# Who evicts the first scores, where expert 0's second weights load, and a new written order

## The chip, the cores and the metric

The kernel runs on one core of a Trainium2 chip. The core has a matmul engine (TensorE, PE in the profile; PEld are its weight loads), VectorE (DVE), ScalarE (ACT), GpSimd (POOL) and SyncE (SP), each with an instruction stream of its own, and 16 DMA engines. The metric is the device time of one execution in microseconds (us). A measurement is the median of several executions; the profile shows one execution by itself.

## The reference

Two blocks follow each other. The first is DeltaNet attention: for 4 x 8 heads of width 48 a state is carried over 768 positions. The second is a mixture of experts over the 3072 rows of 384 that come out: each row goes to the one of 8 experts with the largest logit.

```python
for t in range(S):
    kt, vt, bt = (k_n[:, :, t], v[:, :, t], beta[:, :, t, None])
    y[:, :, t] = np.einsum('bhd,bhde->bhe', q[:, :, t], state)
    v_old = np.einsum('bhde,bhd->bhe', state, kt)
    state = state + bt[:, :, :, None] * np.einsum('bhd,bhe->bhde', kt, vt - v_old)
...
logits = x @ w_gate
expert_idx = np.argmax(logits, axis=1)
...
for e in range(E):
    ...
    h = np.maximum(x_sorted[lo:hi] @ w1[e], 0.0)
    y_sorted[lo:hi] = h @ w2[e]
return (gate_w[:, None] * y).astype(np.float32)
```

k_n is k divided by its norm, gate_w the softmax weight of the chosen expert. All is float32.

## The kernel before

**Attention.** The 768 positions are cut into 12 tiles of 64; the work on one tile is a turn, t = 0 to 11. Within a tile the recurrence is solved by the inverse of a triangular matrix. `scores` (L373) makes the products of keys with keys (into XY, a part of blkA) and with queries (into P, a part of pA), and ScalarE evicts them (L309). Tiles 0 and 1 are handled apart: their products of keys are evicted first into GD, four copies of 32 partitions for each tile, by ScalarE for tile 0 and by VectorE for tile 1 (L311). For the later tiles SP copies GD from XY by DMA. VectorE multiplies P by a mask (L412). `invert(n)` computes the inverses of tiles 2n and 2n+1, all on VectorE: it transposes GD (L437), takes the norms (L445 to L470), keeps their transposed form `nt` (L472), eliminates in steps (L486 to L509) and transposes the result into TT (L517).

A turn is a chain between TensorE and ScalarE. Before it ScalarE scales v by the norms (L530, 16 small instructions a tile, which need `nt`) and copies it to a bank ("pair<-v"). Then come the product of state and keys (L554 into the same bank), the copy to R, the inverse (L583), the copy to Z, the product across the halves (L593), R again, the inverse again (L583), Z again, the update of the state (L607) and its copies to S. Beside the chain stand the output of a tile (L554 with queries, and L639), its eviction to x, its write to HBM (xs), and the logits (L659 transposes, L669, L678, each with an eviction to xT, lgT, lg).

**Routing.** Tiles of 128 rows are routed in groups of 8, 8, 2, 4 and 2. VectorE finds the largest logit (L718 to L735), ScalarE the exponentials (`ex`, L722), TensorE the ranks (L743 and L747, into a bank from which VectorE reads `rk`, L752). `su` (L766) sums `ex`. `listed` turns ranks into the lists of rows of each expert (L796 to L821). With the lists of the first three groups the first 256 rows of expert 0 are gathered (`early_rows`, POOL) and computed early (`early`): transposes (L927), `hidden` (L945) and `second` (L977).

**Experts.** For each of 8 experts: gather, L927, eight blocks of `hidden` with the first weights w1, then `second` with the second weights w2, scaling and scatter. The weights lie in three buffers, taken from the memory of blkA and pA, and SP loads them in three DMAs for w1 and two for w2.

**What sets the order.** All instructions up to the end of the experts are given to a planner (`Plan`) with an engine, an estimated cost, a priority (lower goes first) and a latency. The planner plays the program through with these estimates and writes down the order in which each engine gets its instructions; every engine then works through its list in that order, and waits where an operand isn't there. The dependences that the planner is given only shape this order; the waits on the chip come from the tiles that an instruction reads and writes. The planner also puts in fillers (L1120), matmuls whose result nobody uses, where it expects TensorE to be idle. Constants on top of the file are its estimates and priorities: RUN is how far ahead of their turn the scores are, OUT and LOG how far behind it the output and the logits, MASK the priority of L412, L3 and L4 those of the last lists, APART the turn from which the logits use another bank, ENOUGH the amount of recent matmul work above which no filler is put in.

`cf` is one DMA with all constants, issued by ScalarE; `ents` is a small ScalarE copy of the row numbers out of it. Its latency is 2.5 in the planner.

Of the kernel before, what the change touches and what calls it, by code (L numbers as in the profile page):

```python
# [20 lines left out]
NT = S // C  # L21
# [7 lines left out]
NK = DM // 128  # L29
# [4 lines left out]
FAR = 1 << 20  # L34
RING = 6
AHEAD = 5
RUN = 4.75
PAGE, FILL, STALL = 125, 3.8, 0.8
OUT, LOG = 1.1, 0.2
LATER, OUTL = 8, 1.3  # L40
LISTS, L3, L4, TURN = 9.5, 20.2, 11.05, 11.0
APART = 5
VP, MASK = 0.5, 2.2
WINDOW, WAKE, STAY, PASS = 3.413, 1600, 1750, 8.5
FILLER, ENOUGH, FROM = 0.22, 2500, 36.0
SLACK = 2.0
URGENT = -70

# [170 lines left out]
def tile_kernel(ctx: ExitStack, tc: tile.TileContext, kq, ktok, vtok, betal, wgk, w1, w2, out):  # L219
    nc = tc.nc  # L220
    P = Plan()
# [8 lines left out]
    fc, where = _consts()  # L230
    cf = pool.tile([128, fc.shape[1]], FP32, name="cf")
# [30 lines left out]
    def kb(b):  # L262
        return [("bk", b), ("bk", b + 1)]
# [23 lines left out]
    GD = blk(8)  # L287
# [7 lines left out]
    def dma(eng, o, i):  # L295
        return lambda: eng.dma_start(out=o, in_=i)
# [10 lines left out]
    def copy(eng, o, i, scale=1.0):  # L307
        if eng == "ACT":
            return lambda: nc.scalar.activation(out=o, in_=i, func=AF.Copy, scale=scale)  # L309
        if scale == 1.0:  # L310
            return lambda: nc.vector.tensor_copy(out=o, in_=i)  # L311
        return lambda: nc.vector.tensor_scalar(out=o, in0=i, scalar1=scale, scalar2=None, op0=OP.mult)
# [3 lines left out]
    P.op("DVE", 0.1, lambda: nc.vector.memset(tiny[:], 0.0), w=["tiny"], prio=-99)  # L316
    P.op("ACT", 0.2, lambda: nc.scalar.activation(out=tiny[:], in_=tiny[:], func=AF.Copy), w=["tiny"], prio=-45)
    P.op("ACT", 0.5, dma(nc.scalar, bl[:], betal), w=["bl"], prio=-49, lat=2.5)
    P.op("ACT", 0.5, dma(nc.scalar, cf[:], nc.inline_tensor(fc, name="c_f32").ap()), w=["cf"], prio=-48, lat=2.5)
    P.op("DVE", 0.2, lambda: nc.vector.memset(wg[:], 0.0), w=["wg"], prio=-48)  # L320
    P.op("ACT", 0.5, dma(nc.scalar, wg[:, :, 0:E], wgk), w=["wg"], prio=-40, lat=2.5)
    P.op("DVE", 1.0, lambda: nc.vector.memset(pairs[0][:], 0.0), w=kb(BS), prio=-50)
# [8 lines left out]
    for i in (2, 3, 4, 5):  # L331
        P.op("POOL", 1.85, lambda i=i: nc.gpsimd.memset(kqA[:, 2048 * i : 2048 * i + 2048], 0.0),
             w=kKQ(i) + [("zero", i)], prio=-60)
    for e in range(2):
        r = slice(64 * e + D, 64 * e + 64)
        P.op("SP", 0.6, dma(nc.sync, kqA[r, 2048:4096], kqA[r, 10240:12288]), r=[("zero", 5)], w=[("zero", 1)],
             prio=-40, lat=2.5)
# [25 lines left out]
    def scores(t):  # L363
        v = KQ(t)
        n, u = divmod(t, 2)
        xy = XY[n % 3]

        def run(bank, ks, fs):
            w = C * len(ks)
            for i, f in enumerate(fs):  # L370
                for e in range(2):
                    for x in range(2):
                        nc.tensor.matmul(  # L373
                            bk[bank + e][half(x), i * w : i * w + w].rearrange("p (k c) -> p k c", c=C),
                            lhsT=v[feat(e), 0, x * FQ + f, :],
                            rhs=v[feat(e), ks[0] : ks[-1] + 1, x * FQ + f, :],
                            start=True, stop=True,
                        )

        if t < 2:  # L380
            b = (BY, BZ)[t]
            P.op("PE", 1.15, lambda: run(b, (0,), range(FQ)), r=kKQ(t, (0,)), w=kb(b), prio=t - 95, passes=64, use=770)

            for q in range(4):
                eng = ("ACT", "DVE")[u]
                o = GD[quad(q), :, 16 * u : 16 * u + 16].rearrange("p c (e f) -> p c e f", e=2)
                i = pairs[b // 2][quad(q)].rearrange("p e (f c) -> p c e f", c=C)[:, 32 * (q % 2) : 32 * (q % 2) + 32]
                P.op(eng, 0.5 if u == 0 else 0.6, copy(eng, o, i), r=kb(b), w=[("GD", q, u, e) for e in range(2)], prio=t - 94)
            P.op("ACT", 1.0, copy(
                "ACT",  # L390
                xy[:, :, 16 * u : 16 * u + 16].rearrange("p c (e f) -> p c e f", e=2),
                pairs[b // 2][:].rearrange("p e (f c) -> p c e f", c=C)),
                r=kb(b), w=[("XY", n % 3, u, g) for g in range(2)], prio=t - 60)
            if t == 1:
                P.op("ACT", 0.2, copy("ACT", cnt[:], const("first")), r=["cf"] + kXY(0), w=["cnt"], prio=-55)
            P.op("PE", 1.2, lambda: run(BY, (1,), range(FQ)), r=kKQ(t), w=kb(BY), prio=t - 50, passes=64, use=770)
            P.op("ACT", 1.0, copy("ACT", Pm(t).rearrange("p e f c -> p e (f c)"), pairs[3][:]),
                 r=kb(BY), w=[("P", t % RING)], prio=t - 50)
        else:
            for g in range(2):  # L400
                P.op("PE", 1.1, lambda g=g: run(BY, (0, 1), range(4 * g, 4 * g + 4)), r=kKQ(t), w=kb(BY),
                     prio=t - RUN + 0.01 * g, passes=32, use=770)
                src = pairs[3][:].rearrange("p e (f c) -> p e f c", f=4)
                P.op("ACT", 0.5, copy(
                    "ACT",
                    xy[:, :, 16 * u : 16 * u + 16].rearrange("p c (e f) -> p c e f", e=2)[:, :, :, 4 * g : 4 * g + 4],
                    src[:, :, :, 0:C].rearrange("p e f c -> p c e f")),
                    r=kb(BY), w=[("XY", n % 3, u, g)], prio=t - RUN)
                P.op("ACT", 0.5, copy("ACT", Pm(t)[:, :, 4 * g : 4 * g + 4, :], src[:, :, :, C:]),
                     r=kb(BY), w=[("P", t % RING)], prio=t - RUN)  # L410
        later = const("later").rearrange("p (e c) -> p e c", e=2).unsqueeze(2).to_broadcast([128, 2, FQ, C])
        dve(1024, lambda: nc.vector.tensor_tensor(out=Pm(t), in0=Pm(t), in1=later, op=OP.mult),  # L412
            ["cf"], [("P", t % RING)], t - MASK)
# [235 lines left out]
    def spare(t):  # L649

        return BZ if t < APART or t == NT - 3 else BY if t < NT - 2 else BS if t < NT - 1 else BZ

# [171 lines left out]
    def numbered(o, of, k, r, pr):  # L824

        n = of.shape[1]
        far = fars[:, 0:n]
        dve(n, lambda: nc.vector.tensor_scalar(
            out=far, in0=of, scalar1=0.0, scalar2=float(FAR), op0=OP.is_equal, op1=OP.mult), r, ["fars"], pr)
        dve(n, lambda: nc.vector.scalar_tensor_tensor(  # L830
            out=o, in0=of, scalar=-1.0, in1=far, op0=OP.add, op1=OP.add), r + ["fars"], [k], pr)
# [6 lines left out]
            a[:, NK * F :].rearrange("p (c d) -> p c d", c=NF),  # L838
        )

    def weights(e, pr, behind=()):
        i = e % 3
        a1, a2 = wview(i)
        extra = []
        if e == 0:
            extra = kXY(0) + kXY(1) + [("GL", k) for k in range(2)]
        if e == 1:
            extra = [("P", k) for k in range(RING)]
        if e == 2:
            extra = [k for i in range(2) for k in (("U", i), ("U", i, 21))] + [("GD", q, u, e) for q in range(4) for u in range(2) for e in range(2)] + kXY(2)  # L850
            extra += [("TT", k, h) for k in range(2) for h in range(2)]
        for s in range(NK):
            P.op("SP", SP(524288),
                 dma(nc.sync, a1[:, s, :], w1[e].rearrange("(s p) f -> p s f", p=128)[:, s, :]),
                 r=behind, w=[("w", i, s)] + extra, prio=pr + s)
        for h in range(2):
            P.op("SP", SP(786432),
                 dma(nc.sync, a2[:, 4 * h : 4 * h + 4, :],
                     w2[e].rearrange("(c p) d -> p c d", p=128)[:, 4 * h : 4 * h + 4, :]),
                 r=behind, w=[("w", i, 3 + h)] + extra, prio=pr + 3 + h)  # L860
# [128 lines left out]

    def early_rows():  # L990

        weights(0, 8)
        prepare(0)
        two_tiles = lst[:].rearrange("p (t e) o -> p t e o", e=E)[:, 0:2, 0, :]
        numbered(rows_ei[:], two_tiles[:, :, 0], "rows_ei", ["lst"], -74)
        dve(2, lambda: nc.vector.tensor_copy(out=rows_e[:], in_=two_tiles[:, :, 1]), ["lst"], ["rows_e"], -73)
        xv = XIN[0][0]
        for t in range(2):
            P.op("POOL", 1.0, lambda t=t: gather(xv[:, t * DM : t * DM + DM], rows_ei[:, t : t + 1]),
                 r=["rows_ei"] + [("xs", i) for i in range(18)], w=[("xin", 0, t)], prio=11, lat=2.5)  # L1000

    def early():
        xT, hT = parts(0, EARLY, 0)
        guard = [k for i in range(3) for k in kKQ(i)]
        turned_rows(0, (0, 1), xT, TURN, guard, (BR, BR + 1))
        hidden(0, xT, hT, 21, guard, (2, 0, 3, 1))
        for t in range(2):
            second(0, t, hT, 128 * t, (4, 6)[t], 21.2 + 0.01 * t)
            finish(t, (4, 6)[t], 128, rows_e[:, t : t + 1], rows_ei[:, t : t + 1], "rows_e", 21.2)
# [41 lines left out]
    for i in range(NT + AHEAD + 1):  # L1051
        t = i - AHEAD
# [26 lines left out]
        if i % 2 == 0 and 2 <= i <= NT:  # L1079
            invert(i // 2 - 1)  # L1080
            if i == 2:

                for j in range(2):
                    P.op("POOL", 1.4, lambda j=j: nc.gpsimd.memset(Sbs[j][:], 0.0), r=[("nt", 0)],
                         w=[("S", j, e) for e in range(2)], prio=-15)
                P.op("POOL", 1.85, lambda: nc.gpsimd.memset(kqA[:, 0:2048], 0.0), r=[("nt", 0)],
                     w=kKQ(0) + [("zero", 0)], prio=0)
                last_rows()
    prepare(1)
    numbered(rows_i[:], lst[:, :, 0], "rows_i", ["lst"], -74)  # L1090
    early()

    weights(1, 20, ["rows_i"])
# [125 lines left out]
```

## Time and profile before

| | |
|---|---|
| time, median of 3 runs | 532.78 us (531.04 to 533.56) |
| the profiled execution's own time | 526.99 us |
| its span, first to last instruction | 525.2 us |
| granted TensorE clock, mean | 0.952 |
| TensorE busy | 468.0 us (89%) |
| VectorE, ScalarE, GpSimd busy | 243.7, 191.0, 84.9 us |
| bytes moved by DMA | 63.84 MB |

The start of the first inverse (the first L583 of a turn) in the timeline, in us from the start of the span:

| turn | 0 | 1 | 2 | 3 | 4 | 5 |
|---|---|---|---|---|---|---|
| starts at | 42.52 | 58.09 | 77.27 | 90.50 | 107.29 | 123.42 |

| turn | 6 | 7 | 8 | 9 | 10 | 11 |
|---|---|---|---|---|---|---|
| starts at | 140.99 | 153.65 | 167.87 | 180.84 | 193.69 | 210.66 |

How to read it: busy times are those of one profiled execution, and so are all the times in the timeline. Matmuls overlap with the next one's weights, so a busy TensorE need not be at its peak. "Idle before" is the time in which an engine had nothing to do ahead of an instruction, with the one that released it; "issue" is time for which the profile shows no wait. A float32 matmul of the program appears as two rows in the trace, so counts in the timeline are twice those of the program.

### The profile page before, as it was taken

How to read it: one execution, taken by the hardware profiler on the slowest of the kernel's cores; microseconds unless marked ns; L12 is line 12 of the kernel's file. 1: busy time of each engine (PE TensorE's matmuls, PEld its weight loads, DVE VectorE, ACT ScalarE, POOL GpSimd, SP SyncE). 2: the span in 40 equal slices, each digit the busy share in tenths (PEclk: the TensorE clock that was granted, in tenths of full speed). 3: DMA queues.
4: the chain of work that ended last, by engine and by line, in shares of the span. 5: the costliest groups of instructions: out<-in, count | busy, mean ns of one | idle time of the engine just before them, and what ended most of it. 6: DMA issues, size and time to landing. Idle time of an engine off the chain costs nothing. (4 is left out here: it accounts for less than half of the span.)

```text
span 525.2 us, 15838 instructions
## 1 busy us (share of the span) xinstructions
PE 468.0 (89%) x6850; PEld 321.4 (61%) x6851; DVE 243.7 (46%) x958; ACT 191.0 (36%) x452; POOL 84.9 (16%) x91
## 2 busy tenths in 40 slices
PE   5668898888897898999999999999999999999991
PEld 3557787776786786875755555555555555555550
DVE  3999989999699973251303012212030220121210
ACT  2494978888569974510110110010100111100100
POOL 9100000000010010006510321402301302011020
PEclk9556999899999999999999999999999999999996
DMA  8987365364342434395543413612532301000000
GB/s 202 222 211 201 118 164 161 94 150 131 101 134 94 134 115 152 100 385 176 177 175 121 150 54 139 193 34 107 196 120 82 126 4 46 0 18 30 0 31 13
DMA packets 27849, 63.84 MB, mean 122 GB/s; under 512 B 4026, under 2 KB 16220, under 8 KB 27744
## 3 DMA queue, kind: packets, MB, share of 16 engines
q1 hardware_dynamic: 23376, 52.44, 32.9%
q0 software_dynamic: 3584, 9.44, 5.5%
q10 hardware_dynamic: 816, 0.92, 0.8%
q8 instruction: 54, 0.88, 0.7%
q14 instruction: 19, 0.16, 0.1%
HBM read 49.67 MB, written 11.01 MB: 116 GB/s over the span
## 5 line engine op out<-in xcount | busy, mean ns | idle before, releaser
L945 PE MATMUL pair<-kqA,blkA 128*128 128x416 f32 (+2 forms) x288 | 86.9, 458 | 0.0
L977 PE MATMUL pair<-blkA,kqA 128*128 128x384 f32 x240 | 79.0, 489 | 0.0
L951 DVE TENSOR_SCALAR kqA<-pair 128x416 f32<-128x416 f32 (+2 forms) x36 | 19.6, 543 | 121.7 <-PE pair L945 121.7
L945 PEld LDWEIGHTS pair<-kqA,blkA 128*128 128x128 f32 x288 | 51.2, 190 | 31.3 <-issue 28.3
L977 PEld LDWEIGHTS pair<-blkA,kqA 128*128 128x128 f32 x240 | 45.1, 190 | 33.3 <-issue 3.1
L893 POOL DMA_INDIRECT out<-y,rows_i x30 | 28.7, 956 | 199.7 <-DVE y L1038 122.1
L954 ACT ACTIVATE kqA<-pair 128x416 f32<-128x416 f32 (+2 forms) x36 | 17.2, 478 | 108.9 <-PE pair L945 108.9
L968 ACT ACTIVATE y<-pair,lst 128x384 f32<-128x384 f32 x15 | 8.7, 581 | 128.0 <-PE pair L977 118.3
L373 PE MATMUL pair<-kqA 48*64 48x128 f32 (+1 forms) x896 | 36.3, 319 | 17.4 <-ACT blkA L309 6.0
L945 PE MATMUL pair<-kqA,pA 128*128 128x416 f32 x144 | 51.0, 513 | 0.0
L530 ACT ACTIVATE v<-v,nt 128x48 f32<-128x48 f32 x192 | 48.9, 329 | 3.4 <-DMA v<-in_vtok 1.9
L977 PE MATMUL pair<-pA,kqA 128*128 128x384 f32 x144 | 47.2, 488 | 0.0
L373 PEld LDWEIGHTS pair<-kqA 48*64 48x64 f32 x896 | 29.9, 176 | 23.4 <-ACT pA L309 7.9
L554 PE MATMUL pair<-S,kqA 112*64 112x96 f32 x704 | 35.7, 253 | 9.5 <-ACT S L309 3.1
L945 PEld LDWEIGHTS pair<-kqA,pA 128*128 128x128 f32 x144 | 27.1, 190 | 22.5 <-issue 21.6
L977 PEld LDWEIGHTS pair<-pA,kqA 128*128 128x128 f32 x144 | 27.1, 190 | 20.1 <-issue 1.9
L554 PEld LDWEIGHTS pair<-S,kqA 112*64 112x64 f32 x704 | 30.8, 138 | 12.5 <-issue 4.7
L886 POOL DMA_INDIRECT kqA<-xs,rows_i x30 | 29.8, 994 | 43.2 <-DVE more L1115 26.7
L583 PE MATMUL pair<-R,blkA 32*32 32x48 f32 x1536 | 28.6, 226 | 3.0 <-ACT R L309 1.8
L965 DVE TENSOR_SCALAR y<-pair,lst 128x384 f32<-128x384 f32 x7 | 4.3, 618 | 55.3 <-PE pair L977 55.3
L583 PEld LDWEIGHTS pair<-R,blkA 32*32 32x32 f32 x1536 | 25.3, 146 | 7.3 <-ACT R L309 3.8
L490 DVE TENSOR_TENSOR prod<-blkA 128x16 f32<-128x16 f32 (+7 forms) x96 | 28.8, 300 | 0.0
(136 smaller groups left out, 615.6 us busy)
## 6 DMA issues: line engine op xcount, KB each, us to landing
kqA<-in_kq SPq DMA_DIRECT2D x46, 192.0 KB, 5.2
blkA<-in_w SPq DMA_DIRECT2D x15, 512.0 KB, 4.9
blkA<-in_w SPq DMA_DIRECT2D x10, 768.0 KB, 5.5
v<-in_vtok SPq DMA_DIRECT2D x12, 384.0 KB, 4.1
kt<-in_ktok SPq DMA_DIRECT2D x12, 384.0 KB, 3.6
xs<-x SPq DMA_DIRECT2D x12, 384.0 KB, 2.9
pA<-in_w SPq DMA_DIRECT2D x9, 512.0 KB, 5.6
pA<-in_w SPq DMA_DIRECT2D x6, 768.0 KB, 4.7
```

What stands on the lines that cost most here:

```text
L373: nc.tensor.matmul(bk[bank + e][half(x), i * w : i * w + w].rearrange("p (k c) -> p k c", c=C), lhsT=v[feat(e), 0, x * FQ + f, :], rhs=v[f ...
L490: dve(16 * w, lambda j=j, w=w, pl=pl: nc.vector.tensor_tensor(out=pl, in0=gl[:, 16:32, j : j + 1].to_broadcast([128, 16, w]), in1=u[:, j : ...
L530: P.op("ACT", 0.225, lambda v=v, i=i: nc.scalar.activation(out=v, in_=v, func=AF.Copy, scale=nt[:, 16 * u + i : 16 * u + i + 1]), r=[("nt" ...
L554: nc.tensor.matmul(bk[bank + g][half(x ^ g if first else x), 2 * D * i : 2 * D * i + 2 * D], lhsT=KQ(t)[0 : 64 + D, k, x * FQ + f, :], rhs ...
L583: nc.tensor.matmul(at(BZ, f, e)[quad(q)], lhsT=tt[quad(q), :, 16 * u + 8 * e + f], rhs=R[quad(q), f, e, :], start=True, stop=True, skip_gr ...
L886: nc.gpsimd.indirect_dma_start(out=dst, out_offset=None, in_=xs, in_offset=bass.IndirectOffsetOnAxis(ap=idx, axis=0), bounds_check=N - 1, ...
L893: nc.gpsimd.indirect_dma_start(out=out, out_offset=bass.IndirectOffsetOnAxis(ap=idx, axis=0), in_=src, in_offset=None, bounds_check=N - 1, ...
L945: nc.tensor.matmul(bk[b][:, 0:n], lhsT=a1[:, s, f * 128 : f * 128 + 128], rhs=xT[:, s, :], start=(s == 0), stop=(s == NK - 1))
L951: (lambda f=f, b=b: nc.vector.tensor_scalar(out=hT[:, f, :], in0=bk[b][:, 0:n], scalar1=0.0, scalar2=None, op0=OP.max))
L954: (lambda f=f, b=b: nc.scalar.activation(out=hT[:, f, :], in_=bk[b][:, 0:n], func=AF.Relu)),
L968: (lambda: nc.scalar.activation(out=y[0:n], in_=bk[b][0:n, 0:DM], func=AF.Copy, scale=gate)),
L977: nc.tensor.matmul(bk[b][:, 0:DM], lhsT=hT[:, f, at : at + 128], rhs=a2[:, f, :], start=(f == 0), stop=(f == NF - 1))
```

## The change

Four things are changed.

1. Of the eight copies into GD for tiles 0 and 1 ScalarE does five (all of tile 0, the last of tile 1) and VectorE three; before it was four and four.
2. The planner's latency of the constants' DMA goes from 2.5 to 8.5, so that the order has `ents` behind the first evictions.
3. `weights(0, ...)` is called in two parts. The first weights of expert 0 stay where they were; the second get a later priority and, for the planner, a dependence on the last turn's Z.
4. Constants of the planner are changed. They change no instruction but those above, only the order of nearly all of them on TensorE, ScalarE, VectorE and SP, and how many fillers there are: 46 before, 29 after.

```diff
-RUN = 4.75
+RUN = 4.5
...
-OUT, LOG = 1.1, 0.2
+OUT, LOG = 0.9, 0.2
...
-LISTS, L3, L4, TURN = 9.5, 20.2, 11.05, 11.0
-APART = 5
-VP, MASK = 0.5, 2.2
+LISTS, L3, L4, TURN = 9.5, 11.0, 11.05, 11.0
+APART = 6
+VP, MASK = 0.5, 0.6
...
-FILLER, ENOUGH, FROM = 0.22, 2500, 36.0
+FILLER, ENOUGH, FROM = 0.22, 2200, 36.0
...
-    P.op("ACT", 0.5, dma(nc.scalar, cf[:], nc.inline_tensor(fc, name="c_f32").ap()), w=["cf"], prio=-48, lat=2.5)
+    P.op("ACT", 0.5, dma(nc.scalar, cf[:], nc.inline_tensor(fc, name="c_f32").ap()), w=["cf"], prio=-48, lat=8.5)
...
             for q in range(4):
-                eng = ("ACT", "DVE")[u]
+                eng = "ACT" if u == 0 or q == 3 else "DVE"
...
-                P.op(eng, 0.5 if u == 0 else 0.6, copy(eng, o, i), r=kb(b), w=[("GD", q, u, e) for e in range(2)], prio=t - 94)
+                P.op(eng, 0.6 if eng == "ACT" else 0.7, copy(eng, o, i), r=kb(b), w=[("GD", q, u, e) for e in range(2)], prio=t - 94)
...
-    def weights(e, pr, behind=()):
+    def weights(e, pr, behind=(), of=(0, 1)):
...
-        for s in range(NK):
+        for s in range(NK if 0 in of else 0):
...
-        for h in range(2):
+        for h in range(2 if 1 in of else 0):
...
-        weights(0, 8)
+        weights(0, 8, of=(0,))
...
+    weights(0, 18, [("Z", (NT - 1) % 2)], (1,))
     early()
```

## The prediction

> **What bounds the kernel now.** I read three views in this order: the busy time by stretch, the timeline engine by engine, the DMAs' landings. In the stretches the columns are window, length, then busy us of PE, PEld, DVE, ACT and POOL with instruction counts, granted clock, DMA share, GB/s.
>
> ```profile
> 0.00:42.50 42.50, 24.96 (x484) 19.32 (x485) 32.97 (x127) 22.98 (x59) 15.64 (x19) 0.62 0.93 213
> 42.50:219.70 177.20, 154.61 (x5288) 133.90 (x5286) 148.68 (x675) 135.54 (x326) 8.77 (x10) 0.97 0.43 130
> 219.70:237.00 17.30, 15.93 (x97) 12.52 (x96) 10.17 (x62) 3.80 (x11) 0.00 (x0) 1.00 0.92 333
> 237.00:515.00 278.00, 272.54 (x987) 155.61 (x985) 51.87 (x95) 28.69 (x56) 60.19 (x62) 1.00 0.28 93
> ```
>
> From 219.7 TensorE is full (288.5 of 295.3 us), and the change removes no expert matmul. So what counts is when the first `hidden` matmul (L945) starts; a microsecond won before it is one won at the end, if the weights are there. Before it no engine is full: three engines hand twelve turns to each other, each engine in the written order. These timeline rows (start, length, engine, line, operation, count, idle before and its releaser) show where:
>
> ```profile
> 10.71 0.22 ACT L309 ACTIVATE ents<-cf 128x24 f32<-128x24 f32 x1 [6.54 <-DMA cf<-c_f]
> 13.24 1.30 DVE L437 STREAM_TRANSPOSE blkA<-blkA 128x512 f32<-128x512 f32 x2 [2.14 <-ACT blkA L309]
> 40.49 2.10 PE L373 MATMUL pair<-kqA 48*64 48x128 f32 x32 [1.25 <-issue]
> 42.52 1.51 PE L583 MATMUL pair<-R,blkA 32*32 32x48 f32 x64
> 72.21 0.70 DVE L517 STREAM_TRANSPOSE blkA<-blkA 128x512 f32<-128x512 f32 x1
> 77.27 1.13 PE L583 MATMUL pair<-R,blkA 32*32 32x48 f32 x64
> 94.49 0.79 PE L593 MATMUL pair<-Z,blkA 32*32 32x48 f32 x39 [1.31 <-issue]
> 136.50 0.22 DVE L766 TENSOR_REDUCE su<-ex 128x8 f32<-128x64 f32 x1 [4.82 <-ACT ex L722]
> 136.57 0.81 ACT L309 ACTIVATE R<-pair 128x768 f32<-128x768 f32 x1
> 140.99 1.13 PE L583 MATMUL pair<-R,blkA 32*32 32x48 f32 x64 [0.66 <-DVE rk L752]
> 197.54 1.44 SPq L296 DMA_DIRECT2D blkA<-in_w  x2
> 205.93 0.96 PE L554 MATMUL pair<-S,kqA 112*64 112x96 f32 x17 [1.52 <-issue]
> 210.66 1.13 PE L583 MATMUL pair<-R,blkA 32*32 32x48 f32 x64
> 219.72 1.56 PE L945 MATMUL pair<-kqA,blkA 128*128 128x256 f32 x6
> 235.74 0.44 PE L812 MATMUL pair<-ones_p,vals 128*64 128x128 f32 x4 [0.98 <-DVE vals L804]
> 236.84 10.54 PE L977 MATMUL pair<-blkA,kqA 128*128 128x384 f32 x32
> ```
>
> To be seen: six ScalarE copies stood behind `ents`, which waited for a constant, and the first inversion behind them. The inverse (last L517) lies ready before TensorE takes it (L583): 39.9 to 42.5, 72.9 to 77.3, and in turn 6 the residual R is there at 137.4 but used at 141.0. So order costs more than work. Two stretches more:
>
> ```profile
> 96.00:100.00 4.00, 4.00 (x92) 3.65 (x87) 4.00 (x23) 3.54 (x12) 0.15 (x1) 0.58 0.41 112
> 198.00:202.00 4.00, 3.41 (x147) 2.90 (x145) 3.35 (x10) 1.93 (x4) 0.00 (x0) 1.00 0.97 314
> ```
>
> **What the Trainium skill says.** (1) "TensorE: Matmul & The Clock Gate", Architectural detail: ScalarE and VectorE are strict FIFO. The 6.54 us before `ents` agree. (2) The same page, What's actually happening: the array runs at half or full rate, judged over windows of about 3.4 us. The trace agrees: 0.50 until 44 us, and 0.58 in the stretch at 96, right after a pause of 1.31 us. (3) "Runtime: NRT & Kernel Launch", Terms: an engine's instruction memory is refilled in 16 KiB blocks. The pauses named "issue" inside one run of matmuls (1.31 at 94.49, 1.52 at 205.93) look like waits for that; the trace doesn't show the block. (4) "DMA: Bandwidth & Descriptors", Issuing engines are not separate DMA queues: all share 16 engines. The pauses at 199.4 (0.30) and 205.9 (1.52) fall just behind the second weights issued at 197.54 (DMA share 0.97).
>
> **The change part by part.** The new order per engine can be read from the built program; I walk it with durations of this trace (ScalarE copy of 768 columns 0.81, in a row every 0.72 to 0.84; v scale every 0.225; half of the scores 2.05 at half clock and 1.10 at full; L583 and L593 1.13; L554 1.54; L607 0.94; S pair 1.62; hand-over 0.05 to 0.1).
>
> *Start.* TensorE ends tile 0's scores at about 6.8, tile 1's at 8.27. ScalarE now copies at once: five of 0.6 us, to 9.85, the last with its data since 8.27. VectorE has three of 0.7 from 8.31, to 10.4. First transpose 10.45 for 13.24: VectorE's chain gains 2.8, and its inverse comes at 37.1 for 39.9. But it is not what TensorE waits for alone. The new ScalarE order puts one v scale ahead of tile 2's first eviction; v was issued at 16.77 and landed 6.4 us later (23.2), on DMA engines that were full (share 0.93 in the stretch). That eviction then ends at 24.5 for 23.8, and behind it the chain of scores runs 0.7 to 1.3 us later than before. One half of the scores that stood ahead of the first inverse now stands behind it, so the inverse starts at 40.3 (before 42.52): 2.2 won of 2.8.
>
> *MASK 2.2 to 0.6.* Tile 5's mask now stands inside the second inversion, and tile 5's eviction behind turn 0's Z: VectorE is there at 47.0 and waits until 49 to 51. With its 2.8 us head start used up, the second inverse ends at 73.1 to 74.6 (before 72.9). Nothing won, nearly nothing lost.
>
> *RUN, OUT, APART, fillers (46 to 29, each two rows of the trace).* TensorE now takes turn 2's inverse as soon as it is there, not behind an output and fillers: 73.9 for 77.27, 3.4 won. The next turn gives 2.2 back: v scales stand ahead of Z and S on ScalarE, and the state's product (L554) stands behind the logits, which wait for xT (S ends 84.4, L554 86.1 for 86.47); turn 3 starts at 89.3 for 90.50. Turn 4: 104.1 for 107.29. Turn 5: 118.6 for 123.42, since xT is no longer ahead of L554 and v's DMA is issued earlier (1.93 us of ScalarE waited for it at 120.5). Turn 6: 134.0 for 140.99. Here the wait of `su` for `ex` (4.82) goes: `su` now stands behind the fourth inversion; the logits that stood ahead of the inverse move too. What is late next is `rk` (ranks), which still holds the bank that the inverse writes: VectorE is there at 132.5 to 134. Turn 7: 148.5 for 153.65 (it waits for two logits, 2 us given back). Turn 8: 161.8 for 167.87, turn 10: 187.3 for 193.69, where the ranks stand ahead of L554 (0.7 lost).
>
> *Last turn.* Output 10 now stands ahead of L554 of turn 11 (L554 at 199.0, S at 197.3: 1.7 lost), but no longer between R and the inverse (2.9 won), and the pauses of 0.30 and 1.52 are not in my walk. Turn 11: 201.6 for 210.66. `hidden` starts at 210.5 for 219.72: 9.2 won.
>
> *Second weights of expert 0.* Two DMAs of 768 KB leave 197.54. The first is issued behind tile 10's rows (those wait for the gathers to land), near 205 to 214; the second behind tile 11's rows, near 212 to 221; landing takes 5.5 (their median). On SP the ten weight DMAs of experts 1 and 2 stand behind them, some 1 us later; expert 1's are used at 263. L977 needs them at 228 to 237: about 10 us of cover, which costs nothing; if it were gone, TensorE would stand before L977. What is won is the traffic at 198: between 0 and 1.8 (the two pauses), if it does not make a pause elsewhere.
>
> *L3 20.2 to 11.0.* The list of tiles 18 to 21 comes a little earlier among the `hidden`. Between the last ranks and the last list three `hidden` stand, as before, so the 1.4 us at 235.74 and 236.57 stay: bound from -1.4 to +1, taken 0.
>
> *Pauses.* My walk has none. Before, those from turn 3 on sum to 5.5 (1.31, 0.50, 0.39, 0.71, 0.82, 0.30, 1.52), and the half-clock stretch at 96 costs about 1.7 (4 us at 0.58). The places will differ. The unknown is bounded by 0 (none on the path) and 7.2 (all again); I take the five that the weights' traffic can't explain, 3.7. Sum: 9.2 - 3.7 = 5.5 won.
>
> The profiled execution took 526.99 (span 525.2), the median is 532.78: 1.1% apart, more than half of what I forecast. The walk gives 521.5 against that execution, or 532.8 - 5.5 = 527.3 as a median, which I forecast.
>
> **The rivals.** (A) As worked out, 527.3, own range 523.6 to 530.1. (B) No pause on the path and no clock dip: 9.2 to 11, 522.7. For it: less DMA traffic in the last turns; against it: pauses came about every 15 to 45 us all along. (C) The new waits eat nearly all: ScalarE is 76% busy in the turns, and I found v scales ahead of Z, S or R in six turns, each 0.2 to 1.2, and my starts are sums of many such guesses: some 1.5 left, 531.3. (D) Slower: the clock. Seven of the fillers (14 rows, at 48.06 and 51.47) stood in turn 0, now two. If TensorE falls back to half rate there, a turn costs 4.3 more (L583 and L593 three times 0.4, L607 0.5, L554 0.7, two halves of scores 0.95 each). From two turns on (8.6) the gain is gone and more; two and a half give +5.3, 538. For it: the dips at 48 and 96 each came right after a short pause. Against it: scores now stand inside turn 0, so TensorE has more real work there.
>
> **How the numbers follow.** A 0.52, B 0.18, C 0.18, D 0.12. 0.5% is 2.7 us, about what a measurement of this kernel tells from no change. A and B are faster (0.70), C the same, D slower. The range runs from B's middle, less 0.7 for a last list that comes in time, to just into D: 522 to 534.
>
> **What would show it.** First transpose near 10.5, first L583 near 40.3, `hidden` near 210 to 215, L977 right behind the list with no wait for DMA, no `su` wait at 136. Wrong if clock stretches under 0.7 appear behind 55 us, if VectorE waits over 5 us for tile 5's mask, or if the first `hidden` is not earlier by more than 2.7.

## The result, and the profile after

| | before | after |
|---|---|---|
| time, median of 4 runs each | 531.91 us (530.05 to 533.56) | 524.26 us (523.86 to 527.71) |
| after over before | | 0.9894, 95% interval 0.9852 to 0.9937 |
| the profiled execution's own time | 526.99 us | 524.46 us |
| first inverse of turn 0 | 42.52 | 42.24 |
| first inverse of turn 11 | 210.66 | 209.26 |
| first `hidden` (L945) | 219.72 | 218.51 |
| `second` (L977) | 236.84 | 234.37 |

The change won 7.6 us between the medians, but only 2.5 between the two profiled executions: that of before lay 4.9 below its median, that of after on it. The ratio in the table, 0.9894, stands for 5.6 us. The stretches of the kernel after, cut at the same events as those of before (columns as there):

```profile
0.00:42.24 42.24, 22.91 (x452) 17.17 (x453) 32.45 (x126) 22.49 (x58) 15.61 (x19) 0.64 0.98 207
42.24:218.51 176.27, 151.60 (x5288) 131.50 (x5284) 148.34 (x680) 137.09 (x329) 8.78 (x10) 0.96 0.44 128
218.51:234.37 15.86, 15.47 (x102) 12.27 (x95) 10.34 (x60) 3.73 (x10) 0.00 (x0) 1.00 0.90 335
234.37:512.50 278.13, 272.69 (x988) 155.86 (x987) 51.29 (x93) 28.69 (x56) 60.16 (x62) 1.00 0.29 97
```

The twelve turns (second line) take 176.27 for 177.20, with the same 5288 rows of matmuls. The stretch with the last lists (third line) takes 15.86 for 17.30, or for 17.12 if that of before is cut at L977 as well. The timeline of the kernel after, where the prediction had its steps:

```profile
25.24 0.33 ACT L530 ACTIVATE v<-v,nt 128x48 f32<-128x48 f32 x1 [7.75 <-DVE prod L486]
26.60 1.98 PE L373 MATMUL pair<-kqA 48*64 48x128 f32 x32 [5.46 <-ACT pA L309]
42.24 1.51 PE L583 MATMUL pair<-R,blkA 32*32 32x48 f32 x64
95.66 0.55 PE L593 MATMUL pair<-Z,blkA 32*32 32x48 f32 x22 [1.74 <-issue]
139.16 0.23 DVE L752 TENSOR_TENSOR rk<-pair,cnt 128x72 f32<-128x72 f32 x1 [4.35 <-PE pair L747]
196.89 0.77 PE L593 MATMUL pair<-Z,blkA 32*32 32x48 f32 x35 [1.25 <-issue]
211.42 0.50 SPq L296 DMA_DIRECT2D blkA<-in_w  x1
233.26 0.44 PE L812 MATMUL pair<-ones_p,vals 128*64 128x128 f32 x4
234.37 10.54 PE L977 MATMUL pair<-blkA,kqA 128*128 128x384 f32 x32
```

To be seen: ScalarE stands 7.75 us in front of the first scale of v, with tile 2's first eviction behind it, and TensorE stands for that eviction. The releaser named (VectorE's `prod`) had long been done; the wait ends when v has landed (recorded at 25.16). The wait of VectorE at `su` (4.82 before) is gone, and one of 4.35 at `rk` has come. The pauses named "issue" are there as before. The last list (L812) no longer waits 0.98.

**What the pauses are.** In the view of the DMAs one queue is of the kind "instruction": q8, 54 packets and 0.88 MB in both kernels, 16 KB a packet. It has a packet every few microseconds while the turns run: 42 between 44 and 219, 4.25 us apart on average before and 4.26 after, never under 3.3. Its row on the page after (packets, MB, share of the 16 engines):

```profile
q8 instruction: 54, 0.88, 0.8%
```

Pauses and packets go together. The pause that ends at 95.66 has a packet at 92.7 to 94.2 ahead of it, that at 196.89 one at 194.5 to 195.4, and so for 60.45, 150.26 and 175.13: TensorE goes on 1.3 to 1.6 us after the packet's end, and the next packet starts 1.0 to 1.2 us later. The Trainium skill ("Runtime: NRT & Kernel Launch", Terms) has blocks of 16 KiB; here the packet's size agrees.

The place of the pauses says the same. Number the rows of TensorE in a trace in order of time: matmuls, weight loads and those of its sequencer. In the turns of the 14 profiles (two of the first kernels, twelve below) 166 pauses named "issue" are longer than 0.15 us. Of these, 152 end at row 193 or 194 past a multiple of 256, each 1.2 to 1.7 us after the end of a packet; the other 14 are at most 0.39 us long. Of the 316 waits for ScalarE none ends there. So these pauses are TensorE waiting for its next block of 256 instructions. In the turns of the kernel after they add up to 7.1 us, in those of the kernel before to 6.9. What more instructions cost is tested below.

### The profile page after: what moved, and what is told of

The parts are those of the page before. It is cut to its first block, busy times and chain, and to the rows that moved or that the text cites. A ratio compares the mean times of both kernels' runs of the same rounds, so it can differ in the third digit from the quotient of the medians.

```text
span 522.6 us, 15767 instructions
## 1 busy us (share of the span) xinstructions
PE 462.7 (89%) x6816; PEld 316.8 (61%) x6817; DVE 242.4 (46%) x957; ACT 192.0 (37%) x453; POOL 84.9 (16%) x91
## 5 line engine op out<-in xcount | busy, mean ns | idle before, releaser
L945 PE MATMUL pair<-kqA,blkA 128*128 128x416 f32 (+2 forms) x288 | 87.0, 458 | 0.0
L977 PE MATMUL pair<-blkA,kqA 128*128 128x384 f32 x240 | 79.0, 489 | 0.0
L945 PEld LDWEIGHTS pair<-kqA,blkA 128*128 128x128 f32 x288 | 51.3, 190 | 31.5 <-issue 28.4
L977 PEld LDWEIGHTS pair<-blkA,kqA 128*128 128x128 f32 x240 | 45.2, 190 | 33.3 <-issue 3.1
L954 ACT ACTIVATE kqA<-pair 128x416 f32<-128x416 f32 (+2 forms) x36 | 17.2, 478 | 108.8 <-PE pair L945 108.8
L373 PE MATMUL pair<-kqA 48*64 48x128 f32 (+1 forms) x896 | 36.2, 309 | 20.1 <-ACT pA L309 9.8
L945 PE MATMUL pair<-kqA,pA 128*128 128x416 f32 x144 | 51.0, 513 | 0.0
L977 PE MATMUL pair<-pA,kqA 128*128 128x384 f32 x144 | 47.2, 489 | 0.0
L373 PEld LDWEIGHTS pair<-kqA 48*64 48x64 f32 x896 | 29.0, 165 | 26.2 <-ACT pA L309 12.0
L945 PEld LDWEIGHTS pair<-kqA,pA 128*128 128x128 f32 x144 | 27.2, 190 | 22.5 <-issue 21.6
L977 PEld LDWEIGHTS pair<-pA,kqA 128*128 128x128 f32 x144 | 27.1, 190 | 20.1 <-issue 1.9
```

What stands on the lines that cost most here:

```text
L373: nc.tensor.matmul(bk[bank + e][half(x), i * w : i * w + w].rearrange("p (k c) -> p k c", c=C), lhsT=v[feat(e), 0, x * FQ + f, :], rhs=v[f ...
L945: nc.tensor.matmul(bk[b][:, 0:n], lhsT=a1[:, s, f * 128 : f * 128 + 128], rhs=xT[:, s, :], start=(s == 0), stop=(s == NK - 1))
L954: (lambda f=f, b=b: nc.scalar.activation(out=hT[:, f, :], in_=bk[b][:, 0:n], func=AF.Relu)),
L977: nc.tensor.matmul(bk[b][:, 0:DM], lhsT=hT[:, f, at : at + 128], rhs=a2[:, f, :], start=(f == 0), stop=(f == NF - 1))
```

## The experiments

They were measured in three groups, each on a chip of its own; there the kernel before takes 536.97 to 537.83 (medians), some 5 more than in the first measurement. About 1.9 to 3.3 us of that is a pause of TensorE in the first `hidden` of expert 1 (250 to 272), which all twelve profiles show, of old and new order alike, and the two of the first measurement do not; its cause stays open. Ratios are to the kernel before in the same group, and all differences below are between medians. In kernels with an added line the line numbers are one higher than in the text.

**1. The kernel before, repeated.**

> The kernel before once more, unchanged: what does its time scatter by, and do the pauses named "issue" stay where they are? Every theory expects a ratio of 1.000 within 0.4%. If before's profiled execution (526.99 against a median of 532) was only a lucky draw, single executions of the one program lie between 526 and 534, and another profile of it shows `hidden` starting later than 219.72 by most of the difference, with other pauses or a longer half-clock stretch. If instead profiling itself makes it quicker, the profiled execution lies below all the others again.

Measured: 536.32 (534.08 to 541.63, 22 executions), ratio 0.9978 (0.9952 to 1.0004). `hidden` started at 224.94 in its profile. So one program gives `hidden` 5.2 us apart, and one profile can't show a difference of 3 us; a ratio within about 0.3% of 1 is nothing. Profiling as such does not make it quicker: the profiled execution took 537.40, above the median.

**2 to 4. One part at a time in the kernel before.** The planned order of before is kept, and single instructions are put elsewhere in it; the third takes the new constants with the code of before.

```diff
 # start alone: the copy of the fourth quarter of tile 1 by ScalarE, right behind those of tile 0
+copy("ACT" if q == 3 else eng, o, i)
+put(M["gd", 1, 3], M["gd", 0, 3])
+put(M["ents"], M["cnt"])
 # second weights alone
+put(M["w2", 0, 0], M["xs", 10])
+put(M["w2", 0, 1], M["xs", 11])
 # constants alone
-RUN = 4.75
+RUN = 4.5
...
-OUT, LOG = 1.1, 0.2
+OUT, LOG = 0.9, 0.2
...
```

> The kernel before with the start alone: ScalarE does five of the eight copies into GD, and `ents` stands behind them; nothing else is moved. Theory Start (the gain of the change comes from the start): first transpose near 10.5 to 11, first inverse 2 or more earlier than 42.5, and this is kept to the end: 3 to 6 us faster. Theory Order (the gain comes from the new order of the later work): the first inverse comes up to 2.8 earlier here too, since no scale of v stands ahead of tile 2's first eviction, but the turns after it wait for the next inversion, which VectorE finishes up to 2.8 earlier as well; between 0 and 2.8 us faster. Theory Traffic (the gain comes from the weights' later loads): within 1 us of before.

> The kernel before with the two DMAs of expert 0's second weights moved behind the rows of tiles 10 and 11 on SP, nothing else. Theory Traffic: the pauses near 199 and 206 go, and 1.8 us or more are won, up to the whole 5. Theories Order and Start: between 1 slower and 1 faster, pauses elsewhere, L977 still without a wait for DMA since it starts near 236 and the second DMA lands by about 225.

> The kernel before with the planner's constants alone (RUN, OUT, L3, APART, MASK, ENOUGH): the new order without the new start and with the second weights where they were. Theory Order: 4 to 8 us faster, most or all of what the change brings, the stretch from the first `hidden` to L977 near 15.9. Theory Start: within 2 us of before, since the first inversion still begins at 13.2. Theory Traffic: within 2 us of before.

Measured: start 535.67, ratio 0.9976 (0.9955 to 0.9997); weights 535.48, 0.9971 (0.9947 to 0.9996); constants 535.05, 0.9956 (0.9931 to 0.9980). Beside the repeat (536.32) these are 0.65, 0.84 and 1.27, none of them clear of the repeat's own interval. No part alone brings what the whole brings, which speaks against Start, Traffic and Order, each taken as the only cause: each falls short of what its theory forecast for its own part (3 to 6, at least 1.8, and 4 to 8). With the start alone the first inverse is at 40.85. With the late weights alone the pauses near 199 and 206 are gone, as Traffic had it, and one of 0.59 stands at 196.99. The stretch from `hidden` to L977 is 15.85 with the new constants, and 17.12 or 17.13 in the four profiles with the old ones: the one piece that repeats to 0.01. But the constants alone also pull the second weights to 195.71, right behind the first, and there TensorE pauses for 3 us:

```profile
195.71 1.76 SPq L296 DMA_DIRECT2D blkA<-in_w  x3
203.27 1.55 PE L812 MATMUL pair<-ones_p,vals 128*64 128x128 f32 x12 [3.00 <-issue]
```

**5 to 8. The changed kernel, repeated, and with a part taken back.**

```diff
 # start undone
+copy(("ACT", "DVE")[u], o, i)
+put(M["gd", 1, 3], M["gd", 1, 2])
+put(M["ents"], M["gd", 0, 0])
+put(M["gd", 0, 0], M["ents"])
 # second weights early again
+put(M["w2", 0, 1], M["xs", 9])
+put(M["w2", 0, 0], M["xs", 9])
 # v's latency in the planner
-prio=t - 3.5, lat=4.0 if t < 2 else None
+prio=t - 3.5, lat=8.0 if t < 2 else None
```

> The changed kernel once more, unchanged, so that it stands beside its own variants. Theory Order: about 0.989 of the kernel before, as measured first. Theory Sum (start, weights and constants each bring little, and the first four runs drew a good share of luck): 0.990 to 0.995, since the parts alone measured 0.9976, 0.9971 and 0.9956 against a repeat of the same kernel at 0.9978.

> The changed kernel with its start undone: VectorE does the fourth copy of tile 1 again and `ents` stands ahead of the first copy again; all other instructions stay in the new order. Theory Start: most of the gain is lost, 3 us or more slower than the changed kernel. Theories Order and Sum: first transpose near 13.2, first inverse near 42.5 to 44, and at the end 0 to 2.5 us slower than the changed kernel, since the scores arrive late through the scale of v in any case.

> The changed kernel with the two DMAs of expert 0's second weights moved ahead again, behind the rows of tile 9 on SP; all else in the new order. Theory Traffic: 2 us or more slower than the changed kernel, with pauses of TensorE between 195 and 206. Theories Order and Sum: within 1.5 us of it.

> The changed kernel with the planner told that the first two tiles of v take 8.0 to land instead of 4.0. TensorE's order stays the same; on ScalarE the first scale of v moves from ahead of tile 2's first eviction to behind tile 3's first (and some scales of the next turns shift). If that scale's wait for v (7.75 us idle on ScalarE at 25.24) is what ate the win of the start: ScalarE evicts tile 2's first at about 17, the scores run 1 to 3 us earlier, first inverse near 40.3 instead of 42.2, and 1 to 2.5 us are won at the end. If the turns after it absorb it: within 0.7 us of the changed kernel.

| | time (range) | ratio to before | first inverse | turns 10 to 11 | `hidden` |
|---|---|---|---|---|---|
| repeat | 530.77 (529.04 to 535.18) | 0.9880 (0.9829 to 0.9930) | 40.28 | 17.1 | 220.43 |
| start undone | 531.58 (530.95 to 534.70) | 0.9895 (0.9850 to 0.9940) | 40.06 | 18.2 | 219.48 |
| weights early | 533.95 (531.28 to 539.25) | 0.9945 (0.9912 to 0.9979) | 40.6 | 19.0 | 223.51 |
| v at 8.0 | 530.61 (526.74 to 531.77) | 0.9851 (0.9804 to 0.9898) | 39.2 | 16.9 | 218.18 |

The first result repeats: 6.2 us faster, theory Order's number, though the interval reaches into Sum's 0.990 to 0.995. *Start:* undone, it costs 0.8, less than these runs can tell, and the first inverse is no later (40.06, where theories Order and Sum had 42.5 to 44). The first scale of v on ScalarE in the timeline of the repeat shows why:

```profile
23.24 0.33 ACT L530 ACTIVATE v<-v,nt 128x48 f32<-128x48 f32 x1 [5.58 <-DVE X L498]
```

And with the start undone:

```profile
23.03 0.33 ACT L531 ACTIVATE v<-v,nt 128x48 f32<-128x48 f32 x1 [2.41 <-DVE X L499]
```

ScalarE is ready 3.0 us earlier with the new start and waits 3.2 us longer: in both the wait ends near 23, which fits the landing of v, and the scores go on from there. Theory Start falls. *v at 8.0:* TensorE's order is the same, and ScalarE now takes tile 2's first eviction at 19.83 (forecast 17). The first inverse comes 1.1 earlier, but at the end 0.2 is left, less than these runs can tell. The wait for v ate the win of the start, and yet to take it away brings nothing.

*Weights:* early again, they cost 3.2 us, as theory Traffic had it for this kernel; Order and Sum allowed 1.5. Part of it is in the last turn. From the first inverse of turn 10 to that of turn 11 the five profiles with early weights (before, its repeat, start alone, constants alone, and this one) take 17.0, 18.7, 20.3, 20.5 and 19.0, mean 19.1; the seven with late ones (two of them below) 16.4 to 18.2, mean 17.0. Between the two profiles compared here `hidden` is 3.1 later: 1.8 of it is this turn, and 1.3 is there at turn 10 already, before these weights leave, so that it can't come from them. The stretch from 197.5 to 203.5 of the kernel before:

```profile
197.50:203.50 6.00, 5.41 (x168) 4.36 (x164) 3.91 (x11) 3.91 (x5) 0.00 (x0) 1.00 0.91 305
```

The same of the kernel after:

```profile
197.50:203.50 6.00, 5.85 (x178) 4.76 (x171) 3.85 (x11) 3.58 (x5) 0.00 (x0) 1.00 0.09 31
```

And the timeline of SP and TensorE with the weights early again (L660 transposes x for the logits):

```profile
198.87 1.09 SPq L297 DMA_DIRECT2D blkA<-in_w  x2
205.53 0.33 PE L660 MATMUL pair<-cf,x 128*128 128x128 f32 x1 [1.72 <-issue]
```

The DMA share (last column but one) is 0.91 with the weights there and 0.09 without. Behind them the block of instructions comes late: with early weights one interval between its packets there is 5.8 to 6.9 us (before: 196.9 to 203.7), with late ones, in the same place, 3.5 to 3.9. In three of the five TensorE has just gone on from a pause (at 199.43 before, 197.08 with the constants alone, 199.16 here); the next packet starts only 3.5 to 4.3 us later, and the pauses that follow are 1.52, 3.00 and 1.72. Intervals of 5.6 to 6.7 also occur elsewhere, without these weights.

Taken together, the variants show which parts need each other. The new order with early weights stands at 0.9956 (constants alone) and 0.9945 (weights early), the late weights in the old order at 0.9971, and both together, without the new start, at 0.9895: 5.4 of the 6.2 us.

**9 and 10. Few or many instructions for the same work.** The changed kernel, with useless matmuls on zeros behind the first inverse of turns 1 to 10: the same columns, in 12 or in 32 matmuls.

```diff
+def dummy():
+    for k in range(12):    # or 32
+        q = k % 4
+        nc.tensor.matmul(pairs[BZ // 2][quad(q), 1, DM : DM + 128],    # or 48
+            lhsT=zeros[quad(q), 0:32], rhs=zeros[quad(q), 0:128], ...)
```

> The changed kernel with useless work on TensorE behind the first inverse of turns 1 to 10: 12 matmuls of 32x32 by 128 columns on zeros, about 1.1 us a turn by the rate of the inverse (64 rows of 48 columns in 1.13). It is the partner of a_many, with the same columns in fewer instructions. TensorE waits there for ScalarE's copy of Z in most turns, so that between 0 and 1.1 us a turn shows: 0 to 11 us slower than the changed kernel.

> As a_few, but the same columns in 32 matmuls of 48 columns: 80 instructions more in each of ten turns (a matmul is two rows, each with its weight load). Theory Refill (in the turns TensorE is held by the refill of its instructions, one block of 16 KB at a time, at least 3.4 us apart in the trace): 800 instructions are some 3 refills more, 45 instead of 42 in the turns, and the turns run 5 to 13 us longer than in a_few. Theory Waits (the pauses named issue are chance, and the turns last as long as their chain of TensorE and ScalarE): within 2 us of a_few.

Measured: few 536.64 (533.30 to 541.31), ratio 0.9991 (0.9967 to 1.0015); many 553.38 (549.18 to 554.13), 1.0283 (1.0237 to 1.0328). The useless matmuls in the view of groups (busy us, mean ns of one; idle before), and the queue of instructions in that of the DMAs. Few:

```profile
L1134 PE MATMUL pair<-zeros 32*32 32x128 f32 x240 | 9.1, 268 | 1.1 <-issue 1.1
```

```profile
q8 instruction: 56, 0.92, 0.7%
```

Many:

```profile
L1134 PE MATMUL pair<-zeros 32*32 32x48 f32 x640 | 10.0, 207 | 4.6 <-issue 4.6
```

```profile
q8 instruction: 59, 0.97, 0.8%
```

The useless matmuls keep TensorE busy 0.9 us longer with the many, and the kernel takes 16.7 longer (12.7 at `hidden` between the profiles: 225.65 and 238.31). Theory Waits, with its 2 us, falls. The packets count the instructions: 480 more (matmuls and weight loads) are 2 blocks more than 54, 1280 are 5, which agrees with 256 a block.

The time splits as follows. These are the stretches from the first inverse to `hidden`, few and many:

```profile
41.96:225.65 183.69, 158.86 (x5528) 136.73 (x5525) 147.83 (x680) 137.52 (x329) 8.77 (x10) 0.97 0.42 122
40.56:238.31 197.75, 165.04 (x5929) 143.28 (x5925) 149.18 (x683) 138.17 (x329) 8.77 (x10) 0.94 0.38 114
```

The few are 5.9 us slower than the changed kernel by the ratios (forecast 0 to 11). The many take 14.1 longer than the few in this stretch, a little above Refill's 5 to 13. Pauses named "issue" are 6.5 of it (15.6 against 9.1) and waits for ScalarE 1.6, short gaps 0.3 less. TensorE is busy 6.2 longer: 0.9 is the useless matmuls, and in the other 5.3 the same work runs longer, while the granted clock is lower (0.94 for 0.97; 0.50 at 116 to 120). So theory Refill is shown for less than half; whether the lower clock follows from the pauses or came by chance is not shown.

**11. L3 taken back in the changed kernel.**

```diff
-LISTS, L3, L4, TURN = 9.5, 11.0, 11.05, 11.0
+LISTS, L3, L4, TURN = 9.5, 20.2, 11.05, 11.0
```

> The changed kernel with L3 at 20.2 again; on TensorE only one product of the list of tiles 18 to 21 moves behind the last ranks. If L3 is what shortens the stretch from the first `hidden` to L977 (17.12 in all profiles with the old constants, 15.86 with the new ones), it is 17.1 here and the time 1.3 longer than the changed kernel. If it is the rest of the order there (the ranks and the first three products of the list stand two `hidden` earlier): 15.9 and no more than 0.3.

Measured: 531.20 (530.19 to 533.84), and the stretch is 15.86. So it is not L3; it is the rest of the new order there, in which the last list has its operands when TensorE comes to it (no wait of 0.98 before L812).

**12. v at 8.0, and the first weights of expert 0 later too.**

```diff
+put(M["w1", 0, 2], M["xs", 9])
+put(M["w1", 0, 1], M["xs", 9])
```

> The variant with 8.0 for v, and the second and third DMA of expert 0's first weights moved behind the rows of tile 9 as well. If the pause of 1.0 to 1.4 near 196 comes from their traffic (issued near 190), it goes, and up to 1.2 is won; if the refill that it waits for was not late (its packets were 3.4 to 3.7 apart), the pause stays or moves, and the time is within 0.7 us. Slower by 1 or more if the first `hidden` waits for them.

Measured: 531.09 (526.05 to 533.37), ratio 0.9863 (0.9806 to 0.9919). With less traffic there the interval of the packets ahead of the pause near 196 shrinks from 5.7 (repeat of after) to 4.7 and the pause from 1.16 to 0.63, but nothing is won at the end. No variant beats the changed kernel by more than these runs can tell.

## Why the prediction was right, and where its steps were not

The forecast, 527.3 as a median, lies 3.0 above the measured one, and "faster" was right. The size came partly by luck, as *The sum* shows, and two of its three signs of being wrong appeared: the clock fell under 0.7 behind 55 us (0.64 and 0.51 from 96 to 104), and `hidden` came only 1.2 earlier in the first pair of profiles. Two readings were wrong: the trace does show the block of instructions, and the clock of 0.50 "until 44 us" begins at 10.6, with 1.00 before. Its steps came out thus.

*Start.* "First transpose 10.45": 11.11, since the third copy of VectorE and the fifth of ScalarE waited 0.72 and 0.87 for each other. "The inverse starts at 40.3": 42.24 in the first profile and 40.28 in the second. The working had v land at 23.2; it landed at 25.2 and 23.2. "2.2 won of 2.8" is wrong all the same: in the order of the changed kernel the first inverse stands at 40.06 even with the old start. There, as the prediction also had it, one half of the scores stands behind the inverse that stood ahead of it: six halves (L373, 128 columns) run before it, against seven in the kernel before and with the constants alone (42.59). That half, and not the copies, makes the inverse early in the changed kernel. In the old order the new start alone does bring something, 40.85.

*MASK.* As forecast: the second inverse, ready at 72.9 before, is ready at 74.3 (forecast 73.1 to 74.6), and VectorE waits 0.79 for tile 5's eviction at 50.50, less than was feared.

*RUN, OUT, APART, fillers and the last turn.* This is the part that failed. The walk had turns 2, 4, 6, 8 and 11 at 73.9, 104.1, 134.0, 161.8 and 201.6; they came at 75.65, 108.08, 139.44, 167.51 and 209.26. For turn 6 the forecast named `rk` as next, with VectorE there at 134: it waited until 139.16. From turn 0 to turn 10 the four profiles with the old order take 151.2 to 154.2 (mean 152.7), the eight with the new one, without those of few and many, 150.6 to 156.2 (mean 153.1). The waits that the walk removed are gone, and the turns are no shorter, because others came. TensorE's waits for ScalarE from the first inverse to `hidden` are 12.7 to 14.1 in the four and 15.8 to 17.6 in the eight; its pauses named "issue" are 6.9 to 10.3 and 7.1 to 11.3 (means 8.9 and 8.6), no more than before. The largest single change is the update of the state, which waits for Z (engine, who waits, for whom: us, times, longest), before and after:

```profile
PE pair L607 <- ACT Z L309: 3.1, 4, 1.1
PE pair L607 <- ACT Z L309: 5.8, 7, 1.4
```

The fillers took 17.2 us of TensorE in the turns before and 10.4 after; it fits that part of their time has become waits. Waits for ScalarE are what rival C named; that C's v scales ahead of Z make them was not tested.

*Pauses.* Here stands the mis-sized term: "I take the five that the weights' traffic can't explain, 3.7", which also leaves out the 1.7 that the prediction itself had put on the half clock. From turn 3 on the named pauses of the kernel after are 1.74, 0.63, 0.20, 0.76, 0.15 and 1.25, together 4.7. The clock was at half for 6.8 us from 97.1 and for 3.4 us from 117.6: up to 5.1 more, reckoned as the prediction did it for 96 to 100. `hidden` came 8.0 later than in the walk (218.51 for 210.5), and it came late in three places: 1.9 at the first inverse; 5.1 from turn 3 (90.67 for 89.3) to turn 5 (125.08 for 118.6), where both half-clock stretches and the pauses of 1.74 and 0.63 lie; and 2.1 in the last turn, with the pause of 1.25. How much of each is pause, clock or wait for ScalarE was not separated. The prediction treated the pauses as chance that recurs beside the walk. Their places are not chance, since they stand at the ends of blocks; how long each is changes from one execution to the next. That blocks come 4.25 us apart before and after follows from equal counts and nearly equal times and shows no limit by itself; single intervals go down to 3.3.

*Second weights.* "Costs nothing" is right: L977 waits for no DMA. The gain, "between 0 and 1.8", is 2.0 by the mean of the profiles of the last turn, whose ranges overlap; in times 0.8 in the old order, not clear of noise, and 3.2 in the new, where the weights taken back land on the last turn again.

*L3.* Taken as 0, bounds -1.4 to +1: the stretch is 1.26 shorter, but through the order as a whole, not through L3.

*The sum.* Between the profiles: 1.2 at `hidden` and 1.26 in the last list are the 2.5 won. The walk's 5.5 is thus refuted for the profile that was walked. The forecast then set it against the median, and that fitted by luck: the profile that was walked had been a quick one of its program. Between the two repeats, profile against profile, `hidden` to `hidden` is 4.5 (224.94 to 220.43), itself less than the 5.2 by which one program differs from itself. Last turn 2.0, last list 1.26 and start 0.7 to 0.8 make 4.0 of the 5.6 to 7.6 measured; the parts measured alone make 2.8, and order and late weights together 5.4. So the gain is mostly that of order and late weights in combination; why they bring more together than apart was not taken apart further.

## What to carry to other kernels

Before moving waits about in a stretch of many small matmuls, count its instructions and the packets of the instruction queue, and number the matmuls and weight loads: pauses that return every 256 rows are waits for instructions, and a new order did not shorten them here (6.9 to 10.3 us before, 7.1 to 11.3 after). Look, too, at what stands where a wait or a filler was taken away: here it was another wait for ScalarE. It paid to move a large load that was not needed for 20 us behind the dense stretch, but clearly so only in the new order (3.2 us; 0.8 in the old one). And before a profile of one execution is walked step by step for a few microseconds, take a second one of the same kernel: here `hidden` moved by 5.2 between two.

## What was not expected of the hardware

TensorE's instructions come as DMA packets of 16 KB, 256 instructions each, among the packets of the data: 0.9 to 2.1 us a packet, at least 3.3 us apart, and 5.8 to 6.9 apart when two loads of 768 KB are in flight. Where TensorE runs out of them it stands until 1.2 to 1.7 us after a packet's end: 7 to 11 us in the turns of a kernel of some 530 us. 800 small instructions more, with 0.9 us more of TensorE work, cost 16.7 us; in the profiles 6.5 of 14.1 us were such pauses, and 5.3 the other work running longer at a lower granted clock.
